# Turning two norms of a transformer block by DMA transposes instead of TensorE, with two-operand work freed for DVE

## The chip, the core and the metric

The kernel runs on one core of a Trainium2 chip. The core has TensorE (PE, matrix products, with weight loads shown apart as PEld), VectorE (DVE), ScalarE (ACT), GpSimd (POOL) and SyncE (SP, which here only issues DMAs). Every engine works through its own queue in order; they wait for each other through semaphores. TensorE writes to PSUM, the other engines read PSUM (POOL does not) and SBUF. The metric is the device time of one execution in microseconds.

## The reference

One transformer block on 2048 rows `x` of width 512, with a condition `c` that gives six vectors (shift, scale and gate for each of two halves):

```
mod = silu(c) @ w_mod                       # sa, ca, ga, sb, cb, gb
h = layernorm(x) * (1 + ca) + sa
q = h @ wq                                  # 32 heads of 128
p = softmax(q @ k^T / sqrt(128))            # the last 512 of 2048 cached keys
x = x + ga * ((p @ v) @ wo)
h = layernorm(x) * (1 + cb) + sb
x = x + gb * ((gelu(h @ w_gate) * (h @ w_up)) @ w_down)    # hidden width 1376
```

All inputs and outputs are float32.

## The kernel before

**Numbers.** A float32 value is kept as two float16 tiles, `high` (the rounded value) and `low` (the rest), and a product is three float16 matmuls: high x high, high x low, low x high. Making such a pair is an ACT copy to float16 and a subtraction. To fit float16's range every operand is scaled by its largest absolute value. For each group of two heads these maxima of four weights are *crossed* between partitions: `h_send` (L663) writes the 128 x 4 maxima to a small DRAM tile `most`, `spread_max` (L667) reads all 512 values back into every partition (tile `sa`), reduces them to four (`top`), scales them (`iv`) and takes the reciprocals (`av`). There are 29 such crossings, 28 for heads and one for the feed forward's weights; the first five sets of maxima go through TensorE instead.

**Work.** The 2048 rows are four groups (`qg`) of 512, and two pairs of groups (`p`). `acc` (16 tiles of 128 rows) is the running result. The attention runs 128 iterations (16 groups of heads x 4 row groups x 2 heads), each with scores (`psS`), the softmax, 512 DMA transposes in all from `pp` to `pT`, the product with `v` (`psO`) and with `wo` (`psW`), added to `acc`. From the third head group on, projections use a Strassen-Winograd scheme of seven products instead of eight for a pair of row groups, with the operand sums `T1` to `T4` beside the blocks `B11` to `B22`. The feed forward does the same: 20 units (besides the first pair's f = 0 and 1, which are done plainly), each a pair `p` and a hidden tile `f` of up to 128 columns, seven products of six matmuls into two `psS` tiles, then gelu, the gate, a split into `hid`, and the down projection into `psO`, `psW` or `psQ`, added to `acc`. The units of the first pair with f = 2 to 7 come first; the second pair's first unit is the seventh. Each unit also needs its weights loaded, scaled, summed (`S1` to `S4`) and split (`aw`), and these sums and splits are fixed on POOL.

**The second norm.** For a row group: `ln2_stats` (L1360) takes mean and variance, `ln2_norm` (L1363) writes the normalised rows in float32 to the tiles `N2` (in place of tiles no longer used, so the trace calls them `T` or `B`), and `ln2_chunk` (L1369) turns four 128 x 128 blocks on TensorE into a `psQ` bank, then applies scale and shift into `FULL`, with columns now on partitions. `ln2_high` and `ln2_low` split it into the views of `f_view` (L1354). For groups 1 to 3 `FULL` lives in one of two buffers of the tag `p32` (in the trace `hf`); for group 1 and group 3 these stay taken until `sums_a` and `sums_b` (L1800, L1811) have made the pair's sums and splits from them. The table `P1` (L1843) puts the second pair's norms, chunks and sums beside the units f = 2, 3 and 4 of the first pair.

**Order.** Nothing is issued at once. Every call notes an operation with its cost, its operands and, for some, two possible engines (`either`, L167); `tt` (L963) is a two-operand instruction that POOL or DVE can do, `affine` (L966) one that ACT or DVE can do. `issue` (L412) then plays the whole program in a model: it ranks the operations by how far from the end they have to be done, plays them forward, and repeats this 8 times and then with random shifts (drawn for every operation of the list in turn), stretch by stretch; the best play gives each queue its order and each operation its engine. In the model, a two-operand DVE instruction whose operands lie in SBUF, and any POOL instruction, take a shared lock; where both engines are possible, such an instruction on DVE is charged a penalty `SHY` of 1500 ns when engines are compared:

```
mine = max(t, shared[e] if kinds[e][1] else 0.0) + kinds[e][0] + (e == "DVE" and kinds[e][1]) * self.SHY
```

SP's queue is planned too, so loads and DMA transposes stand in one order. Every instruction is issued at L444, so the profile's rows are told apart by engine and tile.

Of the kernel before, what the change touches and what calls it, by code (L numbers as in the profile page):

```python
# [89 lines left out]
class Weaver:  # L90
# [159 lines left out]
    def play(self, at, users, span, keep, cut):  # L250
# [22 lines left out]
        def sooner(n, e, t):  # L273

            kinds = self.ops[n][4]
            mine = max(t, shared[e] if kinds[e][1] else 0.0) + kinds[e][0] + (e == "DVE" and kinds[e][1]) * self.SHY
            for o, kind in kinds.items():
                s = max(free[o], ready[n], shared[o] if kind[1] else 0.0)
                if o != e and s + kind[0] + (o == "DVE" and kind[1]) * self.SHY < mine:
                    return max(s, t) + 1.0  # L280
            return None

# [169 lines left out]
def adaln_block(ctx: ExitStack, tc: tile.TileContext, x, k_cache, v_cache, wq, wo,  # L452
# [17 lines left out]
    def small(pool, cols_, bufs=3, name="sm"):  # L470
        return pool.tile([P, cols_], F32, name=name, tag=name, bufs=bufs)
# [31 lines left out]
    def b_tile(p, nm, shape=(P, 2, 2, N), dtype=F16):  # L503
        return left1.tile(list(shape), dtype, name=f"{nm}_{p}", tag=f"{nm}_{p}", bufs=1)
# [30 lines left out]

    MV, RS, NMR, LNP, LNF = {}, {}, {}, {}, {}

    def ln_stats(key, src, j):
        if j == 0:
            MV[key] = base.tile([P, 4, 2], F32, name="mv", tag="mv", bufs=4)  # L540
            RS[key] = small(base, 4, 4, "rs")
        st = small(base, 6, 2, "bnst")
        nc.vector.bn_stats(st, src)
        nc.vector.bn_aggr(MV[key][:, j, :], st)
        if j == 3:
            ve = small(base, NC, 2, "ve")
            nc.gpsimd.tensor_tensor(ve, MV[key][:, :, 1], eps_t[:, :NC], op=OP.add)
            nc.gpsimd.tensor_tensor(RS[key], ve, eps_t[:, NC:], op=OP.pow)
            nm = NMR[key] = small(base, 4, 4, "nmr")
            nc.gpsimd.tensor_tensor(nm, MV[key][:, :, 0], RS[key], op=OP.mult)  # L550
            nc.gpsimd.tensor_scalar(nm, nm, -1.0, 1.0, op0=OP.mult, op1=OP.mult)
# [109 lines left out]
            IV[kh], AV[kh] = iv[:, i:i + 1], av[:, i:i + 1]  # L661

    def h_send(which, m):  # L663
        t = DG[which[0]] = dram.tile([P, 4], F32, name="most", tag="most", bufs=3)
        nc.sync.dma_start(t, m[:, 0:4])

    def spread_max(t, top):  # L667
        w = right.tile([P, N], F32, name="sa", tag="sa", bufs=1)
        nc.sync.dma_start(w, t.rearrange("p a -> (p a)").partition_broadcast(P))
        r = small(base, 4, 2, "top")  # L670
        nc.vector.tensor_reduce(r, w.rearrange("p (k a) -> p a k", a=4), op=OP.max, axis=AX.X)
        iv, av = small(base, 8, 5, "iv"), small(base, 8, 5, "av")
        nc.vector.tensor_scalar(iv[:, 0:4], r, 1e-30, ROUND / top, op0=OP.max, op1=OP.mult)
        nc.vector.reciprocal(av[:, 0:4], iv[:, 0:4])
        return iv, av

# [592 lines left out]
    def ff_scalars(part):  # L1269
        ab, t = ffs[:, 6:7], ffs[:, 7:8]  # L1270
        if part == 0:
            FS["iv"], av = spread_max(DG.pop("f"), WS)
            nc.vector.tensor_scalar_mul(ffs[:, 0:2], av[:, 0:2], 0.5)
            nc.vector.tensor_scalar_mul(ffs[:, 2:3], av[:, 2:3], 0.5)
            nc.vector.tensor_scalar(ab, FS["iv"][:, 3:4], WS, 1e-25, op0=OP.mult, op1=OP.max)
        iv = FS["iv"]
        if part == 1:
            nc.vector.tensor_scalar(ffs[:, 3:4], ab, iv[:, 0:1], 2.0 / HS, op0=OP.mult, op1=OP.mult)
            nc.vector.tensor_scalar(t, ab, iv[:, 0:1], 2.0, op0=OP.mult, op1=OP.mult)
            nc.vector.tensor_scalar(ffs[:, 5:6], ab, iv[:, 1:2], 4.0 * HID / HS, op0=OP.mult, op1=OP.mult)  # L1280
            nc.vector.tensor_scalar(ffs[:, 5:6], ffs[:, 5:6], iv[:, 2:3], t, op0=OP.mult, op1=OP.mult)
        if part == 2:
            nc.vector.tensor_scalar_mul(t, t, HID)
            nc.vector.reciprocal(ffs[:, 4:5], t)
            nc.vector.reciprocal(ffs[:, 8:9], ab)
            nc.vector.tensor_scalar(cols[:, 8:16], cols[:, 8:16], ffs[:, 8:9], HS, op0=OP.mult, op1=OP.mult)

    s = max(s, 2 * (NIT - 16))
# [49 lines left out]

    N2, FULL, FB, FRAW, AW, WD, WGU, PGU, HID_T, RT, UV, PX = ({} for _ in range(12))
    PLAIN = 2  # L1340
    SLOTS = ("q", "q", "q", "k16", "A1", "A1", "raw2", "raw2")
    SBUFS = {"q": 3, "k16": 1, "A1": 2, "raw2": 2}
    WDTAG = ("kT", "v", "wo", "kT", "kT", "v", "v", "wo", "wo", "oT", "oT")
# [14 lines left out]
        return t[:, 0, c % 2, :], t[:, 1, c % 2, :]  # L1358

    def ln2_stats(qg, j):  # L1360
        ln_stats(("2", qg), acc[4 * qg + j], j)

    def ln2_norm(qg, j):  # L1363
        if j % 2 == 0:
# [450 lines left out]
        f_low(p, c, "T4")  # L1815

    def chunk2(qg, c):
        ln2_chunk(qg, c)
        ln2_high(qg, c)
        ln2_low(qg, c, nc.vector)  # L1820

# [16 lines left out]
    for c in range(2):  # L1838
        sums_b(0, c)
    down_put(0, (0, 1))  # L1840


    P1 = {2: [(ln2_stats, 2, j) for j in range(4)] +  # L1843
          [(ln2_norm, 2, j) for j in range(4)] + [(chunk2, 2, c) for c in range(4)],
          3: [(ln2_stats, 3, j) for j in range(4)] +
          [(ln2_norm, 3, j) for j in range(4)] + [(chunk2, 3, c) for c in range(4)],
          4: [(sums_a, 1, c) for c in range(2)] + [(sums_b, 1, c) for c in range(2)]}
    WDS = list(range(PLAIN, NF))
    left = {(p, h): 2 if h < NF // 2 else 1 for p in range(2) for h in range(NF // 2 + 1)}
# [75 lines left out]
```

## Time and profile before

| what | us |
|---|---|
| median of 3 runs | 1657.21 (1657.04 to 1657.30) |
| the profiled execution | 1657.58 |
| its span | 1655.8 |
| PE busy in the span | 1642.4 |
| POOL, DVE, ACT busy | 1305.0, 1289.3, 1216.6 |

The terms of the page: `out<-in` names the tiles that an instruction writes and reads, with shapes as partitions x elements, then count, busy time and the mean of one in ns. Behind a bar stands the idle time of the engine just before these instructions, and what ended it. A row of a table by stretches gives the stretch, its length, each engine's busy time with its number of instructions, TensorE's granted clock, the mean busy share of the DMA engines and the GB/s they moved. A row about one tile gives the shortest, median and longest duration in ns and the first and last start. In a list in order of time, a line merges neighbours of one kind: start, length, engine. A row of waits gives the total, the count and the longest.

### The profile page before, as it was taken

How to read it: one execution, taken by the hardware profiler on the slowest of the kernel's cores; microseconds unless marked ns; L12 is line 12 of the kernel's file. 1: busy time of each engine (PE TensorE's matmuls, PEld its weight loads, DVE VectorE, ACT ScalarE, POOL GpSimd, SP SyncE). 2: the span in 40 equal slices, each digit the busy share in tenths (PEclk: the TensorE clock that was granted, in tenths of full speed). 3: DMA queues.
4: the chain of work that ended last, by engine and by line, in shares of the span. 5: the costliest groups of instructions: out<-in, count | busy, mean ns of one | idle time of the engine just before them, and what ended most of it. 6: DMA issues, size and time to landing. Idle time of an engine off the chain costs nothing.

```text
span 1655.8 us, 24293 instructions
## 1 busy us (share of the span) xinstructions
PE 1642.4 (99%) x7732; PEld 764.5 (46%) x7732; DVE 1289.3 (78%) x2381; ACT 1216.6 (73%) x2418; POOL 1305.0 (79%) x1097
## 2 busy tenths in 40 slices
PE   8999999999999999999999999999999999999999
PEld 4444444444444444444444444444444444444455
DVE  7777787878787788788999887888887956656557
ACT  5987797777787777888778777787878876545451
POOL 5999986868586878787768889999977898784682
PEclk9999999999999999999999999999999999999999
DMA  7676697878787778999999997788877712101111
GB/s 241 128 144 130 135 157 143 152 138 149 144 143 140 153 136 157 186 196 194 196 200 205 189 167 148 147 175 179 168 129 158 144 28 64 42 25 51 42 45 52
DMA packets 686289, 228.61 MB, mean 138 GB/s; under 512 B 596432, under 2 KB 663056, under 8 KB 686160
## 3 DMA queue, kind: packets, MB, share of 16 engines
q1 hardware_dynamic: 686160, 227.05, 69.1%
q8 instruction: 61, 1.00, 0.3%
q14 instruction: 68, 0.56, 0.1%
HBM read 78.98 MB, written 5.38 MB: 51 GB/s over the span
## 4 chain that ended last, share of the span: by engine, by line
PE 91%; ACT 2%; POOL 2%; DVE 2%; DMA 1%; SPq 1%; issue 1%; DVEq 0%; POOLq 0%; ACTq 0%
PE psS L444 31%; PE psW L444 23%; PE psO L444 21%; PE psQ L444 17%; SPq L444 1%; DVE st L444 1%; DVE acc L444 1%; DMA pT<-pp 1%; ACT p L444 0%; POOL pp L444 0%; POOL B L444 0%; DMA wm<-in_w_mod_dram 0%; POOL aw L444 0%; ACT T L444 0%; DMA raw<-in_B_w_up_dram 0%
## 5 line engine op out<-in xcount | busy, mean ns | idle before, releaser
L444 POOL TENSOR_TENSOR pp<-p,pp 128x1024 f16<-128x1024 f32 x256 | 545.9, 2132 | 212.8 <-ACT pp L444 97.3
L444 ACT ACTIVATE p<-psS,st,es 128x512 f32<-128x512 f32 x512 | 393.4, 774 | 187.7 <-DVE st L444 186.8
L444 DVE SCALAR_TENSOR_TENSOR acc<-psW,st,acc 128x512 f32<-128x512 f32 x496 | 367.2, 742 | 79.8 <-PE psW L444 77.7
L444 PE MATMUL psW<-wo,oT 128*128 128x512 f16 x1536 | 416.3, 379 | 0.0
L444 PE MATMUL psS<-kT,q 128*128 128x512 f16 x1536 | 379.1, 379 | 2.0 <-ACT q L444 2.0
L444 PE MATMUL psO<-pT,v 128*128 128x512 f16 x1536 | 377.1, 379 | 0.3 <-DMA pT<-pp 0.2
L444 DVE TENSOR_REDUCE st<-psS 128x2 f32<-128x1024 f32 x256 | 312.5, 1221 | 60.0 <-PE psS L444 59.6
L444 ACT ACTIVATE pp<-p 128x1024 f16<-128x1024 f32 x256 | 271.0, 1059 | 3.7
L444 PEld LDWEIGHTS <-q 128*128 128x128 f16 x1536 | 149.9, 98 | 182.1 <-ACT q L444 2.6
L444 PEld LDWEIGHTS <-v 128*128 128x128 f16 x1536 | 150.0, 98 | 181.3 <-DMA pT<-pp 1.2
L444 PEld LDWEIGHTS <-oT 128*128 128x128 f16 x1536 | 150.2, 98 | 180.1 <-DVE oT L444 0.5
L444 PEld LDWEIGHTS <-aw 128*128 128x128 f16 (+1 forms) x840 | 84.2, 100 | 95.1 <-issue 2.0
L444 ACT ACTIVATE oT<-psO 128x512 f16<-128x512 f32 x128 | 76.1, 594 | 66.2 <-PE psO L444 66.1
L444 PE MATMUL psQ<-T,S 128*128 128x512 f16 x504 | 123.3, 379 | 0.0
L444 PE MATMUL psQ<-B,A 128*128 128x512 f16 x480 | 119.6, 381 | 0.1
L444 PE MATMUL psS<-T,aw 128*128 128x512 f16 (+1 forms) x480 | 116.9, 379 | 0.0
L444 DVE SCALAR_TENSOR_TENSOR oT<-psO,oT 128x512 f16<-128x512 f32 x128 | 88.0, 688 | 30.9 <-ACT oT L444 30.6
L444 PEld LDWEIGHTS <-A 128*128 128x128 f16 x696 | 68.3, 98 | 83.3 <-issue 2.3
L444 PEld LDWEIGHTS <-S 128*128 128x128 f16 x672 | 65.8, 98 | 79.3
L444 ACT ACTIVATION_READ_ACCUMULATOR p<-psS,st,es 128x1 f32 x512 | 101.0, 197 | 0.0
L444 POOL TENSOR_TENSOR q<-h,q 128x512 f16<-128x512 f32 x84 | 97.5, 1161 | 2.0 <-ACT q L444 1.8
L444 DVE TENSOR_REDUCE mx<-raw 128x1 f32<-128x512 f32 x128 | 84.2, 674 | 15.6 <-DMA raw<-in_A_wq_dram 9.1
(211 smaller groups left out, 2295.6 us busy)
## 6 DMA issues: line engine op xcount, KB each, us to landing
raw<-in_A_k_cache_dram SPq DMA_DIRECT2D x32, 256.0 KB, 3.9
raw<-in_A_wq_dram SPq DMA_DIRECT2D x32, 256.0 KB, 3.7
raw<-in_A_v_cache_dram SPq DMA_DIRECT2D x32, 256.0 KB, 3.3
raw<-in_A_wo_dram SPq DMA_DIRECT2D x32, 256.0 KB, 3.2
pT<-pp SPq DMA_TRANSPOSE x512, 3.3
sa<-most SPq DMA_DIRECT2D x29, 256.0 KB, 3.8
raw<-in_B_w_gate_dram SPq DMA_DIRECT2D x24, 256.0 KB, 3.1
raw<-in_B_w_up_dram SPq DMA_DIRECT2D x24, 256.0 KB, 3.4
```

Of the source, the lines that this page charges most:

```text
L444: made[n] = real(*a, **k)
```

## The change

Three things are changed.

1. The norms of row groups 2 and 3 are turned by DMA. `turned_norm` normalises into a `p32` tile (scaled by 512 through `RS`, which `ln_stats` multiplies when `big` is set), and splits the row tile into a high and a low float16 half. `turned` issues two DMA transposes for each row tile, straight into the tiles that later hold the high and low parts. `turned_chunk` adds the two turned halves with scale and shift back into `FULL`: an `affine` on the low half, then a DVE instruction that multiplies the high half and adds. The chunk's split follows as before and overwrites the turned halves. `ffs[:, 9:13]` holds the scale for it.
2. The penalty `SHY` counts only for operations noted before `nc.calm`, the first of the feed forward's, so the feed forward's two-operand work goes to DVE or POOL by time alone.
3. The crossing's DRAM tile is 4 x 128 instead of 128 x 4, so a partition's four maxima are written as four single values, and each partition then reduces four runs of 128 neighbours. The scaling into `iv` goes from DVE to POOL.

```diff
@@ sooner
-            mine = max(t, shared[e] if kinds[e][1] else 0.0) + kinds[e][0] + (e == "DVE" and kinds[e][1]) * self.SHY
+            mine = max(t, shared[e] if kinds[e][1] else 0.0) + kinds[e][0] + (e == "DVE" and kinds[e][1]) * (self.SHY if n < self.calm else 0.0)
...
-                if o != e and s + kind[0] + (o == "DVE" and kind[1]) * self.SHY < mine:
+                if o != e and s + kind[0] + (o == "DVE" and kind[1]) * (self.SHY if n < self.calm else 0.0) < mine:
@@ ln_stats
+            if big:
+                nc.gpsimd.tensor_scalar(RS[key], RS[key], HS, 1.0, op0=OP.mult, op1=OP.mult)
@@ h_send, spread_max
-        t = DG[which[0]] = dram.tile([P, 4], F32, name="most", tag="most", bufs=3)
-        nc.sync.dma_start(t, m[:, 0:4])
+        t = DG[which[0]] = dram.tile([4, P], F32, name="most", tag="most", bufs=3)
+        nc.sync.dma_start(t.rearrange("a p -> p a"), m[:, 0:4])
...
-        nc.sync.dma_start(w, t.rearrange("p a -> (p a)").partition_broadcast(P))
+        nc.sync.dma_start(w, t.rearrange("a p -> (a p)").partition_broadcast(P))
...
-        nc.vector.tensor_reduce(r, w.rearrange("p (k a) -> p a k", a=4), op=OP.max, axis=AX.X)
+        nc.vector.tensor_reduce(r, w.rearrange("p (a k) -> p a k", a=4), op=OP.max, axis=AX.X)
...
-        nc.vector.tensor_scalar(iv[:, 0:4], r, 1e-30, ROUND / top, op0=OP.max, op1=OP.mult)
+        nc.gpsimd.tensor_scalar(iv[:, 0:4], r, 1e-30, ROUND / top, op0=OP.max, op1=OP.mult)
@@ ff_scalars
+            nc.vector.tensor_scalar_mul(ffs[:, 9:13], cols[:, 8:12], ffs[:, 8:9])
@@ the feed forward
+    nc.calm = len(nc.ops)
...
-        ln_stats(("2", qg), acc[4 * qg + j], j)
+        ln_stats(("2", qg), acc[4 * qg + j], j, qg in TURNED)
+
+    TURNED = (2, 3)
+
+    def turned_norm(qg, j):
+        if j % 2 == 0:
+            t = b_tile(0, N2TAG[qg][j // 2], (P, 2, 2, 2, N // 2))
+            N2[qg, j], N2[qg, j + 1] = t[:, 0], t[:, 1]
+            RT["norm"] = right.tile([P, 2, N], F32, name="hf", tag="p32", bufs=2)
+        n, t = RT["norm"][:, j % 2, :], N2[qg, j]
+        nc.either((S_, V), lambda o: ln_norm(("2", qg), n, acc[4 * qg + j], j, o))
+        n = n.rearrange("p (a n) -> p a n", a=2)
+        nc.scalar.activation(t[:, :, 0, :], n, AF.Copy)
+        tt(t[:, :, 1, :], n, t[:, :, 0, :], OP.subtract)
+
+    def turned(qg, j):
+        for half in range(2):
+            nm = (("B11", "B21"), ("T4", "B22"))[qg % 2][half]
+            d = ff_b(qg // 2, nm).rearrange("p a c n -> p (a c) n")
+            nc.sync.dma_start_transpose(d[:, :, j * P:(j + 1) * P], N2[qg, j][:, half].rearrange("p a n -> p (a n)"))
+
+    def turned_chunk(qg, c):
+        if c % 2 == 0:
+            RT["full"] = right.tile([P, 2, N], F32, name="hf", tag="p32", bufs=2)
+        full = FULL[qg, c] = RT["full"][:, c % 2, :]
+        a, b = ffs[:, 9 + c:10 + c], colB[2][:, c:c + 1]
+        hi, lo = f_view(qg, c)
+        affine(full, lo, a, b)
+        nc.vector.scalar_tensor_tensor(full, hi, a, full, op0=OP.mult, op1=OP.add)
@@ chunk2 and P1
-        ln2_chunk(qg, c)
+        turned_chunk(qg, c)
...
-          [(ln2_norm, 2, j) for j in range(4)] + [(chunk2, 2, c) for c in range(4)],
+          [(g, 2, j) for j in range(4) for g in (turned_norm, turned)] + [(chunk2, 2, c) for c in range(4)],
...
-          [(ln2_norm, 3, j) for j in range(4)] + [(chunk2, 3, c) for c in range(4)],
+          [(g, 3, j) for j in range(4) for g in (turned_norm, turned)] + [(chunk2, 3, c) for c in range(4)],
```

2 lines of the change are left out of this document (1 added, 1 removed).

## The prediction

> **What bounds the kernel now.** I read the page's first part first, then busy time by stretch, then TensorE's waits in the tail, then the instructions on the tile `ident` (the transposes), then the groups of the stretch in which the changed code runs.
>
> ```profile
> span 1655.8 us, 24293 instructions
> PE 1642.4 (99%) x7732; PEld 764.5 (46%) x7732; DVE 1289.3 (78%) x2381; ACT 1216.6 (73%) x2418; POOL 1305.0 (79%) x1097
> ```
>
> ```profile
> core 0: us, PE busy (x) PEld busy (x) DVE busy (x) ACT busy (x) POOL busy (x), PEclk, DMA share, GB/s
> 0.00:50.00 50.00, 42.42 (x203) 24.88 (x204) 37.91 (x97) 30.76 (x53) 29.70 (x51) 0.93 0.73 216
> ...
> 400.00:600.00 200.00, 200.00 (x928) 90.69 (x927) 161.59 (x307) 151.44 (x308) 144.07 (x109) 1.00 0.78 146
> ...
> 1300.00:1350.00 50.00, 49.40 (x245) 24.39 (x244) 40.34 (x79) 41.65 (x77) 42.74 (x42) 1.00 0.51 106
> 1350.00:1400.00 50.00, 50.00 (x247) 24.40 (x245) 28.79 (x43) 36.55 (x67) 43.23 (x52) 1.00 0.14 37
> 1400.00:1450.00 50.00, 49.95 (x234) 22.82 (x233) 32.83 (x42) 27.41 (x50) 40.93 (x42) 1.00 0.20 56
> 1450.00:1500.00 50.00, 49.09 (x227) 22.10 (x226) 29.60 (x40) 25.10 (x47) 38.35 (x44) 1.00 0.11 31
> 1500.00:1550.00 50.00, 50.00 (x234) 23.70 (x232) 31.11 (x42) 27.41 (x54) 29.23 (x37) 1.00 0.14 38
> ```
>
> TensorE is busy in every microsecond of the attention stretches and has a full granted clock there: 928 instructions in 200 us are 0.2155 us each, the pace of a 512-column matmul. It is idle 7.6 us in the first 50 us and about 1.5 us in the feed forward (0.6 us before 1350, 0.9 us after 1450). What it waits for from 1290 us on:
>
> ```profile
> PE psS L444 <- POOL B L444: 0.6, 1, 0.6
> PE psS L444 <- ACT r L444: 0.5, 1, 0.5
> PE psS L444 <- DVE r L444: 0.4, 1, 0.4
> ```
>
> So the kernel is TensorE's queue plus a start and an end. An edit shortens the time by the TensorE work that it takes out, and by no more than 1.5 us through waits in the feed forward; it lengthens the time by every wait that it puts in. Work that leaves DVE, ACT or POOL is worth nothing by itself.
>
> **What the change removes.** `ln2_chunk` transposes row groups 2 and 3 on TensorE, 2 groups x 4 chunks x 4 tiles = 32 instructions. They are these, and one group of four stands between matmuls like this:
>
> ```profile
> L444 PE MATMUL psQ<-ident,T x32: 272/273/328, 1353.3 to 1416.7; 128*128 128x128 f32 x32
> ```
>
> ```profile
> 1355.51 0.65 PE L444 MATMUL psQ<-ident,T 128*128 128x128 f32 x4
> 1356.00 1.24 PE L444 MATMUL psS<-B,aw 128*128 128x512 f16 x5
> ...
> 1358.59 0.60 PE L444 MATMUL psQ<-ident,T 128*128 128x128 f32 x4
> 1359.03 0.38 PE L444 MATMUL psS<-B,aw 128*128 128x512 f16 x1
> ```
>
> The 273 ns of one is its length in a pipeline. Its cost is the distance to the next start: 0.44 us for four here, and 0.49 us for the group at 1355.51. Eight such groups are 3.5 to 3.9 us; most look like the 0.44 one, so I take 3.6 us. No TensorE instruction is added. The profiled execution took 1657.58 us (span 1655.8 us and 1.8 us around it), so with a full queue it would take 1654.0 us; the median of the runs shown is 0.4 us below the profiled one, so the forecast stands against 1657.21 us: 1657.21 - 3.6 = 1653.6 us.
>
> **What it adds in the feed forward.** The rows are from 1350 to 1460 us, where both norms, their chunks and the sums of the second pair run:
>
> ```profile
> L444 DVE TENSOR_TENSOR hid<-r,hid 128x512 f16<-128x512 f32 x14 | 12.2, 880 | 2.0 <-ACT hid L444 1.9
> L444 DVE SCALAR_TENSOR_TENSOR r<-r,ffs 128x512 f32<-128x512 f32 x12 | 11.2, 956 | 0.1
> L444 POOL TENSOR_TENSOR T<-hf,T 128x512 f16<-128x512 f32 x9 | 10.9, 1213 | 1.3 <-DVE r L444 0.6 <-DVE hid L444 0.6
> L444 POOL TENSOR_TENSOR B<-hf,B 128x512 f16<-128x512 f32 x6 | 6.9, 1163 | 1.9 <-DVE hid L444 1.9
> L444 ACT ACTIVATE raw<-raw,ffs 128x512 f32<-128x512 f32 x9 | 6.2, 708 | 0.0
> L444 ACT ACTIVATE T<-acc,nmr,rs 128x512 f32<-128x512 f32 x6 | 4.5, 803 | 0.8 <-POOL nmr L444 0.8
> L444 ACT ACTIVATE T<-hf 128x512 f16<-128x512 f32 x7 | 4.4, 622 | 2.2 <-POOL hf L444 2.2
> L444 ACT ACTIVATE hf<-psQ,cols 128x512 f32<-128x512 f32 x4 | 3.1, 778 | 1.7 <-POOL B L444 1.4 <-PE psQ L444 0.3
> ```
>
> For each of the 8 row tiles `turned_norm` adds an ACT copy (622 ns) and a two-operand subtraction (1163 ns on POOL; on DVE 880 ns in this stretch, 686 ns where nothing held it up, below). For each of the 8 chunks `turned_chunk` keeps the affine, now from SBUF (708 to 803 ns instead of 778), and adds a DVE instruction with two SBUF operands (686 to 956 ns). That is 5.0 us of ACT, 5.5 to 9.3 us for the subtractions and 5.5 to 7.6 us of DVE, over some 75 us. ACT has 36 us idle in the 100 us from 1350, DVE 38 us, POOL 16 us: the sum fits if some of POOL's work goes to DVE, which the removed penalty lets the planner do. On TensorE's path none of it costs anything as long as the second pair's operands are ready in time.
>
> ```profile
> L444 DVE TENSOR_TENSOR hid<-r,hid 128x512 f16<-128x512 f32 x6 | 4.0, 686 | 0.0
> ```
>
> ```profile
> 1354.68 0.78 ACT L444 ACTIVATE hf<-psQ,cols 128x512 f32<-128x512 f32 x1
> ...
> 1362.87 0.81 DVE L444 TENSOR_SCALAR hf<-psQ,cols 128x512 f32<-128x512 f32 x1 [3.56 <-PE psW L444]
> ```
>
> ```profile
> 1409.05 2.28 POOL L444 TENSOR_TENSOR B<-hf,B 128x512 f16<-128x512 f32 x2 [0.63 <-DVE hid L444]
> ...
> 1459.25 1.16 POOL L444 TENSOR_TENSOR T<-hf,T 128x512 f16<-128x512 f32 x1
> ```
>
> **The longer chain.** The norms now go through the two `p32` buffers, which hold the first pair's chunks until its sums are done. They came free for the next chunks at about 1354.7 and 1362.9 us, so the second two norms of group 2 start at about 1363. Estimated from the rows above: two norms, copies and subtractions 5 us, turning 4 us, two chunks of a buffer 5 us; the same again for group 3 gives 28 us, ready at about 1391. The trace of before splits group 3's chunks from 1409 on and finishes the sums' splits at 1460, so the latency fits with some 18 us to spare.
>
> ```profile
> L444 SPq DMA_TRANSPOSE pT<-pp x512: 1231/1326/4018, 42.7 to 1320.1; - x171
> ```
>
> ```profile
> pT<-pp SPq DMA_TRANSPOSE x512, 3.3
> most<-mx SPq DMA_DIRECT2D x28, 2.0 KB, 1.9
> msu<-mall SPq DMA_DIRECT2D x2, 2.0 KB, 3.1
> ```
>
> ```profile
> 1419.92 12.37 SPq L444 DMA_DIRECT2D raw<-in_B_w_down_dram  x3
> ```
>
> The 16 DMA transposes are half as long as the 512 known ones, so each takes between 0 and 1.33 us of SP (I take 0.7) and lands in at most 3.3 us after issue; the DMA engines are used at 0.11 to 0.20 here. A transpose that waits on SP for its subtraction holds back the weight loads behind it, and the loads themselves wait for buffers (three of them across 12.4 us at 1420), which could hold a transpose back; the loads run two units ahead and the chain has its 18 us, so I price both at nothing; if that cover were gone, a transpose behind such a load would cost up to the 12.4 us of that row.
>
> **The crossings.** 29 times, under attention:
>
> ```profile
> L444 DVE TENSOR_REDUCE top<-sa x29: 1061/1080/1159, 160.5 to 1221.8; 128x4 f32<-128x512 f32 x29
> L444 DVE TENSOR_SCALAR iv<-top x29: 134/164/633, 168.3 to 1224.9; 128x4 f32<-128x4 f32 x29
> ```
>
> ```profile
> L444 DVE TENSOR_REDUCE mx<-raw x128: 622/675/687, 15.8 to 1212.8; 128x1 f32<-128x512 f32 x128
> ```
>
> Laid out by kind, the reduction reads neighbours like `mx<-raw`: between no gain and 0.4 us, and I take 0.4. The scaling leaves DVE for POOL, 0.16 us, and the reciprocal on DVE then waits for POOL, behind up to one 1.2 us subtraction. The send now writes 512 single values instead of 128 runs of four; the nearest row that moves single values is `msu<-mall` (3.1 us) against 1.9 us, so it lands 0 to 1.2 us later. The DMA engines are busy enough elsewhere for this to be taken up: 0.78 in the row of 400 to 600. All of it lies under stretches in which TensorE lost nothing in 200 us, and the heads are prepared a group ahead; I price it at nothing, and at -0.2 to +1 us if one crossing comes too late.
>
> **The redrawn order.** The list of operations and DVE's penalty change, so the planner's search draws another order for all queues. The start's 7.6 us of idle can come out otherwise: I allow 1 us either way (the longest waits there are about that), and take 0.
>
> **The rivals.**
> (1) *Waits come back at the second pair* (a wait takes the place of the work removed). DVE empties `psS` and `psW` in order; the three waits quoted above already end on ACT's and DVE's `r`. Each two-operand instruction given to DVE stands ahead of such an emptying for 0.7 to 1.0 us, and five of them that come at the wrong moment return half of the gain: 1653.6 + 2 = 1655.6 us, with 1 to 5 us as its spread. For it speaks DVE's mean of 880 and 956 ns against 686; against it, that TensorE lost only 0.9 us with these.
> (2) *The port that DVE's two-operand instructions and POOL take in turns is full, and the time rises.* In 1350 to 1460 POOL is busy 43.2 + 40.9 + about 8 = 92 of 110 us, and DVE's 26 instructions of the two quoted groups need 18 us even at 686 ns: 110 of 110. The change adds 11 to 17 us. Every POOL instruction moved to DVE returns 1.16 - 0.69, about 0.5 us. If half of the addition isn't returned, 8 us arrive late at the second pair's first unit, whose last splits end at 1460 already with no spare: 1653.6 + 8 = 1661.6 us. It decides from the point where the last `T` split ends later than about 1465. Against it: POOL is busy only 29 us in 1500 to 1550, so weight splits can slide past it.
> The Trainium skill, "SBUF — State Buffer", "Who interferes with whom", says that a DVE instruction with two SBUF inputs and a GpSimd instruction that reads SBUF exclude each other for a whole instruction. The rows agree (686 against 880 ns), and by that rule DVE's idle time is not free for this work: it is what rival 2 works out.
> (3) *The gain is larger*: the 1.5 us of waits go too, since DVE does a subtraction in less time than POOL, or the start comes out 1 us shorter: 1653.6 - 2 = 1651.6 us.
> (4) That the transposes stay on TensorE can't be: the chunks of groups 2 and 3 call nothing that issues them.
>
> **How the numbers follow.** Forecast with a full queue 0.55 (own range 1652.6 to 1654.6), rival 1 0.22, rival 2 0.11, rival 3 0.12. About 0.2% (3.3 us, so below 1653.9 or above 1660.5) is what a measurement of this kernel tells from no change. The forecast lies only 0.3 us beyond that line: two thirds of it, 0.37, and all of rival 3 count as faster, 0.49; the remaining 0.18 and rival 1 are the same, 0.40; rival 2 is slower, 0.11. The range takes in rival 3's centre and rival 1's spread and stops short of rival 2's centre: 1651.6 to 1658.6.
>
> **What would show it.** Right: no `psQ<-ident` after 1345 us, TensorE idle in the feed forward at 2 us or less, its busy time lower by 3 to 4 us, half or more of the `T`, `B` and `ft` subtractions on DVE. Wrong: a wait of `psS` on `r`, `T` or `B` of over 1 us near the second pair (rivals 1 and 2), or a start that differs by more than 1 us from 42.4 us busy in 50.

## The result, and the profile after

| | median us (range) |
|---|---|
| before, run beside it | 1657.12 (1656.26 to 1657.30) |
| the changed kernel | 1783.67 (1782.28 to 1788.34) |
| ratio, 95% interval | 1.077 (1.0754 to 1.0786) |

The change costs 126 us. The profiled execution took 1782.98 us. The page's first part, then its stretches and one crossing in a table by stretches, with the columns as before:

```profile
span 1781.2 us, 24348 instructions
PE 1673.3 (94%) x7700; PEld 766.3 (43%) x7700; DVE 1438.6 (81%) x2642; ACT 1224.1 (69%) x2424; POOL 1035.0 (58%) x857
```

```profile
400.00:500.00 100.00, 93.16 (x418) 41.43 (x417) 77.15 (x146) 68.47 (x142) 54.87 (x40) 0.97 0.79 135
900.00:1000.00 100.00, 85.35 (x384) 37.85 (x383) 74.15 (x137) 66.35 (x135) 53.52 (x36) 0.94 0.88 140
...
1500.00:1550.00 50.00, 50.00 (x234) 22.68 (x232) 39.73 (x57) 35.19 (x68) 29.33 (x35) 1.00 0.31 72
```

The 32 transposes are gone (7700 against 7732) and POOL's work has moved to DVE (1438.6 against 1289.3, 1035.0 against 1305.0), so the change does what it says. But the loss lies under attention, where TensorE had been busy in every microsecond: 418 and 384 matmuls in 100 us, where the full pace is 464. The feed forward is fast again. The added 125.4 us of span (1781.2 - 1655.8) split into 94.5 us more of TensorE's idle time (107.9 against 13.4) and 30.9 us more of its busy time, in spite of 32 fewer instructions.

What TensorE, POOL and DVE wait for (rows of waits over the whole span):

```profile
POOL iv L444 <- DVE top L444: 79.2, 18, 10.4
...
DVE top L444 <- DMA sa<-most: 75.5, 20, 7.6
...
PE psO L444 <- DMA pT<-pp: 34.2, 17, 5.8
...
PE psQ L444 <- DVE q L444: 27.1, 7, 7.7
...
PE psW L444 <- DVE acc L444: 24.6, 15, 3.8
```

Two rows of waits of the kernel before, the second for later:

```profile
DVE mx L444 <- DMA raw<-in_A_wq_dram: 9.1, 5, 2.2
DVE top L444 <- DMA sa<-most: 7.2, 8, 2.2
```

DVE now stands before the crossing's reduction 20 times, for up to 7.6 us, and what DVE should empty meanwhile (`q`, `acc`) is late for TensorE. The transfers, with their median from issue to landing in us, say where this begins:

```profile
most<-mx SPq DMA_DIRECT2D x28, 2.0 KB, 9.5
...
B<-T SPq DMA_TRANSPOSE x12, 2.5
...
T<-T SPq DMA_TRANSPOSE x4, 2.4
```

The crossing's send, 1.9 us before, lands after 9.5 us. One crossing in order of time:

```profile
629.87 0.57 SPq L444 DMA_DIRECT2D most<-mx  x1
...
631.13 2.62 SPq L444 DMA_TRANSPOSE pT<-pp  x2
...
641.34 0.33 SPq L444 DMA_DIRECT2D sa<-most  x1
...
642.21 0.38 PE L444 MATMUL psO<-pT,v 128*128 128x512 f16 x1 [3.35 <-DMA pT<-pp]
...
645.71 0.69 DVE L444 TENSOR_REDUCE top<-sa 128x4 f32<-128x512 f32 x1 [7.61 <-DMA sa<-most]
```

```profile
630.00:634.00 4.00, 4.00 (x21) 1.81 (x19) 3.84 (x10) 2.52 (x6) 1.16 (x1) 1.00 0.79 135
634.00:638.00 4.00, 4.00 (x20) 1.81 (x19) 3.25 (x7) 4.00 (x9) 3.22 (x3) 1.00 1.68 31
638.00:642.00 4.00, 0.86 (x4) 0.20 (x2) 0.11 (x1) 0.88 (x2) 2.93 (x2) 1.00 1.28 63
642.00:646.00 4.00, 3.79 (x18) 1.79 (x19) 0.29 (x1) 0.00 (x0) 0.00 (x0) 1.00 1.48 188
```

SP issues the send at 629.9 and two transposes at 631.1, and then, but for one load, nothing until 641.3: the read of `most` stands next in its queue and waits for the send. The two transposes were issued before that, and still TensorE can use the last one only at 642.2, some 8.5 us after SP was done with it at 633.75; the median of such a transfer is 3.3 us, and the longest of the changed kernel 14.8 us (6.8 before):

```profile
DMA to landing us min/median/max: 3.1/3.3/14.8
```

In the table the last two columns are the share of the DMA engines and the GB/s that they moved. The share is the time that the packets took, added up, so it can pass 1: from 634 to 638 it is the highest of these rows (1.68), with 31 GB/s. Few packets, each of them long, fit a send that does not only land late but holds up other transfers while it does.

### The profile page after: what moved, and what is told of

Read it like the earlier page. It is cut to its first block, busy times and chain, and to the rows that moved or that the text cites. A ratio compares the mean times of both kernels' runs of the same rounds, so it can differ in the third digit from the quotient of the medians.

```text
span 1781.2 us, 24348 instructions
## 1 busy us (share of the span) xinstructions
PE 1673.3 (94%) x7700; PEld 766.3 (43%) x7700; DVE 1438.6 (81%) x2642; ACT 1224.1 (69%) x2424; POOL 1035.0 (58%) x857
## 5 line engine op out<-in xcount | busy, mean ns | idle before, releaser
L444 PE MATMUL psW<-wo,oT 128*128 128x512 f16 x1536 | 474.2, 384 | 25.8 <-DVE acc L444 24.6
L444 PE MATMUL psO<-pT,v 128*128 128x512 f16 x1536 | 409.2, 383 | 37.5 <-DMA pT<-pp 34.2
L444 PE MATMUL psS<-kT,q 128*128 128x512 f16 x1536 | 411.3, 384 | 1.2 <-ACT q L444 1.2
L444 PE MATMUL psQ<-T,S 128*128 128x512 f16 x504 | 144.0, 395 | 27.2 <-DVE q L444 27.1
L444 PE MATMUL psQ<-B,A 128*128 128x512 f16 x480 | 129.2, 380 | 1.2 <-DVE h L444 1.1
L444 PE MATMUL psS<-T,aw 128*128 128x512 f16 (+1 forms) x480 | 121.1, 379 | 0.0
L444 PE MATMUL psS<-B,aw 128*128 128x512 f16 (+1 forms) x360 | 90.0, 379 | 0.0
```

The lines of the kernel that those rows point to most:

```text
L444: made[n] = real(*a, **k)
```

## The experiments

**Part by part.** The first runs take each part alone or leave the suspect out. The crossing's layout alone, in the kernel before:

```diff
-        t = DG[which[0]] = dram.tile([P, 4], F32, name="most", tag="most", bufs=3)
-        nc.sync.dma_start(t, m[:, 0:4])
+        t = DG[which[0]] = dram.tile([4, P], F32, name="most", tag="most", bufs=3)
+        nc.sync.dma_start(t.rearrange("a p -> p a"), m[:, 0:4])
...
-        nc.sync.dma_start(w, t.rearrange("p a -> (p a)").partition_broadcast(P))
-        nc.vector.tensor_reduce(r, w.rearrange("p (k a) -> p a k", a=4), op=OP.max, axis=AX.X)
+        nc.sync.dma_start(w, t.rearrange("a p -> (a p)").partition_broadcast(P))
+        nc.vector.tensor_reduce(r, w.rearrange("p (a k) -> p a k", a=4), op=OP.max, axis=AX.X)
```

> The kernel before with the crossing's new layout alone (4 x 128, single values sent, four runs reduced); scaling on DVE, penalty and norms as before. Theory L (the send of 512 single values lands after 9.5 us in the trace of after, not after 1.9 us as before, and SP, DVE and POOL stand in order behind it): 1735 to 1785 us, the send again near 9 us. Theory S (the penalty's removal reaches the attention, because its operations are noted after the line that sets the border: POOL has 857 instructions instead of 1097, and DVE's extra work delays what empties PSUM): 1655 to 1662 us, late sends or not.

Measured: 1804.84 us against 1657.46, ratio 1.0885 (1.0869 to 1.0901). The next kernel is the changed one with these lines turned back (`iv` stays on POOL):

> The changed kernel with the crossing's old layout (128 x 4), all else as changed: scaling on POOL, penalty off, norms turned. Theory L: 1653 to 1670 us, the send at 2 us, no long waits of DVE on the spread maxima. Theory S: 1730 to 1785 us, with TensorE's waits on DVE's q and acc left as they are.

Measured: 1661.15 us, ratio 1.0019 (1.0009 to 1.0028). The other two parts alone, in the kernel before: the penalty taken off as in the change, and the turned norms with the penalty kept, the old layout and `iv` on DVE.

```diff
-            ... (e == "DVE" and kinds[e][1]) * self.SHY
+            ... (e == "DVE" and kinds[e][1]) * (self.SHY if n < self.calm else 0.0)
+    nc.calm = len(nc.ops)
```

> The kernel before with the penalty off for all operations noted from the feed forward's set-up on, as in the change; nothing else. Theory S: 1700 us or more. Theory L: 1650 to 1668 us; POOL's instructions fall to about 860 as in the changed kernel, and TensorE stays busy all the same, with at most 10 us of waits on DVE.

```diff
-    nc.calm = len(nc.ops)
+    nc.calm = 1 << 30
```

> The kernel before with the turned norms alone: old crossing with its scaling on DVE, penalty on everywhere. Both theories: the prediction's own step, TensorE's queue 3.6 us shorter, 1653.6 us; up to 1657 us if the longer chain brings waits at the second pair, since without DVE's help the subtractions stay on POOL.

Measured: penalty off alone 1671.55 us, ratio 1.0080 (1.0065 to 1.0095); turned norms alone 1671.94 us, ratio 1.0086 (1.0069 to 1.0103). The pages of these two kernels:

```profile
most<-mx SPq DMA_DIRECT2D x28, 2.0 KB, 9.4
```

```profile
most<-mx SPq DMA_DIRECT2D x28, 2.0 KB, 2.1
...
PE 1638.2 (99%) x7700; PEld 760.7 (46%) x7700; DVE 1446.3 (87%) x2642; ACT 1223.9 (74%) x2424; POOL 1035.9 (62%) x857
```

The first row is of the layout alone, the other two are of the change without it. With the layout goes the send's 9.4 us and 147 us; without it both are gone, and the change costs 3.7 us. So the layout makes some 122 of the 126 us. Neither of the other parts gains anything alone: each loses 14 us, and together they lose less than either. The extra 21 us by which the layout alone is slower than the whole change were not taken apart.

**Late or in the way?** The planner's model has a small DMA land some 2.5 us after issue when no other is under way. If the loss comes from queues laid out for an early landing (SP and DVE standing in order behind a late value), a planner that knows of the 8 us lays the reads later and wins most of it back. If the send disturbs other transfers, it can't.

```diff
-                end = bus + 650.0
+                end = bus + 650.0 + 8000.0 * (n in self.slow)
```

with `slow` the sends of `most`, and the same 8000 ns added where the model ranks the operations from the end.

> The changed kernel, whose planner is told that the crossing's send lands 8 us later than it assumes; the sends stay 512 single values. Theory Q (the time is lost because instructions stand in order behind a send that the plan believes landed: SP's read of it ahead of DMA transposes, DVE's reduction, POOL's scaling): 1655 to 1675 us, the sends still at 9 us, few waits of DVE on the spread maxima. Theory D (the sends' many small writes slow the DMA engines and so the transposes themselves, whoever waits): 1730 us or more.

Measured: 1792.80 us, ratio 1.0806 (1.0767 to 1.0845), no better than 1783.67. Its rows of waits:

```profile
DVE mx L446 <- DMA raw<-in_A_wq_dram: 50.1, 11, 10.4
...
DVE top L446 <- DMA sa<-most: 28.4, 12, 5.3
...
PE psW L446 <- DVE acc L446: 41.7, 14, 8.9
...
PE psO L446 <- DMA pT<-pp: 23.3, 11, 4.8
```

DVE's wait for the crossing fell from 75.5 to 28.4 us, as the planner now leaves room. SP's own wait for the send, 70.5 us in the changed kernel, is gone altogether. The time did not fall with them: DVE waits for weight loads instead (50.1 us; 9.1 us before the change). That speaks for transfers in each other's way. What the packets of the trace show, lined up on the issue of every send (all traffic but packets of 16 bytes and less, the mean over 29 sends):

```
us from the send's issue     -4..0   0..4   4..8   8..12   12..16
before, GB/s                   160    123    175     156      151
after, GB/s                    163    110     59      77      201
planner told, GB/s             175     99     44      70      185
longest packet of the other transfers in 4..8 us (median of the 29 sends):
0.59 us before, 2.67 us after, 2.35 us with the planner told
```

From 4 to 12 us after the issue the other transfers move a third to a half of what they moved at that place before. The rate alone would not prove that they are held up, since SP issues little while it stands behind the send. The length of the packets is less open to that: the longest are some four times what they were, also in the kernel where SP no longer waits for the send. The send's own packets are short: in the crossing shown they take up to 9 ns each, all within half a microsecond after 631.0; the long ones are the transposes' of 256 bytes.

**Which writes are slow?** Unread extra sends in the kernel before, beside the crossing's own; they add work and leave none out. In the first kernel every crossing issues three kinds back to back; in the second each crossing issues one, four kinds in turn:

```diff
         nc.sync.dma_start(t, m[:, 0:4])
+        # in turn, each to a DRAM tile of its own:
+        prk: [4, 128]      <- m[:, 0:4]   512 values, 128 neighbours at 4 B
+        prs: [128, 8]      <- m[:, 0:4]   512 values, at 8 B
+        prw: [4, 128 x 16] <- m[:, 0:4]   512 values, at 64 B
+        pro: [1, 128]      <- m[:, 0:1]   128 values, neighbours at 4 B
```

> The kernel before with three more sends at each of the 28 crossings of heads, which nobody reads: prk (512 single values laid out by kind, as in the change), prs (512 single values, a partition's four 8 bytes apart in 32 bytes of its own), pro (128 single values, one kind). If single values cost by their number, prk and prs both land after about 9 us, pro after 2 to 3 us. If it is neighbours from different partitions in one line of DRAM, prk and pro are slow against prs, which lands after about 2 to 4 us. The time itself: 1657 to 1700 us, of no weight.

> The kernel before with one more unread send at each crossing of heads, of four kinds in turn, seven of each: prk (512 single values by kind, neighbours 4 bytes apart in DRAM), prs (512 single values, 8 bytes apart), prw (512 single values, 64 bytes apart), pro (128 single values, 4 bytes apart). In the first probe all three stood behind one another and landed together at 9 to 11 us, which told nothing apart. If the number of values decides: prk, prs, prw near 9 us, pro near 3 us. If neighbours in one line of DRAM decide: prw 2 to 4 us, prk, prs and pro slow. Time between 1700 and 1800 us, of no weight.

Measured, one execution each: 1894.06 us for the first and 1733.91 us for the second. In the first, `pro`, `prs` and `prk` land after 9.2, 9.4 and 10.6 us in the median. The landings in the second:

```profile
most<-mx SPq DMA_DIRECT2D x28, 2.0 KB, 2.1
...
prk<-mx SPq DMA_DIRECT2D x8, 2.0 KB, 9.5
...
prs<-mx SPq DMA_DIRECT2D x7, 2.0 KB, 4.6
...
prw<-mx SPq DMA_DIRECT2D x7, 2.0 KB, 2.6
...
pro<-mx SPq DMA_DIRECT2D x6, 0.5 KB, 9.2
```

In the first kernel the three kinds are issued back to back and all read about alike, so it tells nothing of a kind by itself. The second does. 512 single values cost 2.6 us when each has 64 bytes to itself, and 128 single values cost 9.2 us when they are neighbours. So it is not the number of single values but how closely they are written. Counted by the packets that fall into the same 64 bytes, 1, 4 (the old layout's 16-byte runs), 8 and 16 of them give 2.6, 2.1, 4.6 and 9.2 to 9.5 us: from 4 up the time is about 0.6 us for each. That is a fit to five rows, in which the 64 bytes are a choice; it looks as if packets to the same place in DRAM were written one after the other, which no run shows by itself.

The Trainium skill, "DMA: Bandwidth & Descriptors", "Specifications", says that transfers of less than 512 bytes cost a read-modify-write. By that, the old layout's 16 bytes and the new one's 4 would both pay it; the runs (2.1 against 9.5 us, and 2.6 us for 4 bytes apart from each other) show a difference that this rule alone does not give. Its "Rules for kernel authors" speaks against this change: a non-contiguous last dimension becomes one descriptor per element and should be made contiguous. The changed send is such a case and is slow, but the send of 512 single values 64 bytes apart is one too, and lands in 2.6 us: the count of descriptors alone is not the price.

**The turned norms and the penalty.** What remains is 3.7 us, though each of the two other parts alone loses 14. First the border: in the changed kernel `nc.calm` stands at L1344, but the attention's operations are noted later, by the loop `for i in range(NIT + 4): slot(i)` (L1825); the penalty is off for the attention too. These two kernels set the border behind that loop, the first with the turned norms, the second without:

```diff
-    nc.calm = len(nc.ops)
...
         slot(i)
+    nc.calm = len(nc.ops)
     hooks(
```

> The kernel before with the turned norms, and the penalty off from the feed forward's own operations on (the border noted behind the attention's loop); old crossing, scaling on DVE. If the 12 us that the turned norms alone lose in 1400 to 1500 us come from POOL's share of the subtractions, they shrink to 0 to 3 us and the attention loses nothing: 1652 to 1657 us. If the longer chain through two buffers and SP's queue is what is late, 1662 us or more, as with the turned norms alone.

> The kernel before with the penalty off in the feed forward alone; norms turned on TensorE, old crossing. If POOL's share is what the feed forward's 1.5 us of waits rest on: 1655 to 1657 us. If DVE's added work delays what empties PSUM, as it did in the attention when the penalty was off there (14 us): 1659 us or more.

Measured: with the turned norms 1659.90 us, ratio 1.0014 (1.0005 to 1.0023); without them 1667.06 us, ratio 1.0059 (1.0044 to 1.0074). So taking the penalty off costs 14.1 us where it goes for the attention too and 9.9 us where it goes behind it, and the same freedom in the feed forward is worth 12 us once the turned norms are in (1671.94 to 1659.90).

Where the first two losses lie is seen from TensorE's instructions between 200 and 1300 us, under attention: 5095 before, 5019 with the penalty off everywhere, 5062 with it off in the feed forward alone. At 0.2155 us each that is 16 us, as much as the whole loss of 14, and 7 of the 9.9 us, though in the second kernel the attention keeps its penalty. In the change without the layout it is 5076, some 4 us lost, with the penalty off as in the first. The turned norms have no work there, so they can't be what brings 16 us down to 4: the redrawn order can, or `iv` on POOL, and no run tells these apart.

Why do the turned norms lose? By the prediction's own candidates: the buffers `p32`, the two-operand work, or the new draw of the order. The norms through a tile of their own:

```diff
-            RT["norm"] = right.tile([P, 2, N], F32, name="hf", tag="p32", bufs=2)
-        n, t = RT["norm"][:, j % 2, :], N2[qg, j]
+        n, t = ga, N2[qg, j]
```

> The kernel with turned norms and the penalty off in the feed forward alone, whose norms go through the tile of the attention's gate (free by then) instead of the two p32 buffers. If the p32 buffers make the second pair late (the chain of norms and chunks through the same two buffers), TensorE's loss in 1400 to 1500 us falls from 5.8 us to 2 us or less: 1654 to 1656.5 us. If it is the sheer work on POOL, DVE and ACT, nothing changes: 1658 to 1662 us.

> The turned norms with the penalty on everywhere, through the gate's tile instead of the p32 buffers. If the buffers are the cause: from 1672 us to 1655 to 1660 us. If it is POOL's work (eight more subtractions, kept there by the penalty): 1668 to 1675 us.

Measured: 1659.78 us, ratio 1.0015 (1.0006 to 1.0025), where the penalty is off in the feed forward, and 1670.60 us, ratio 1.0078 (1.0061 to 1.0095), with the penalty. Both are where they were: the buffers are not the cause. The work itself, with the penalty on: the low halves left out, so no subtraction and no instruction on DVE that adds the halves (the second pair is then computed from rows rounded to float16, and only the high half is transposed), and the turned norms for one group only:

```diff
-        tt(t[:, :, 1, :], n, t[:, :, 0, :], OP.subtract)
...
-        affine(full, lo, a, b)
-        nc.vector.scalar_tensor_tensor(full, hi, a, full, op0=OP.mult, op1=OP.add)
+        affine(full, hi, a, b)
```

> The turned norms with the penalty on, without the low halves: no subtraction when a row tile is split, only the high half turned, and the chunk made from it by the affine instruction alone, so the second pair is computed from rounded rows. What is left is the chain: norm, copy, DMA transpose, chunk, through the same buffers and SP's queue. If the 16 added two-operand instructions are what makes the second pair late (alone the turned norms lost 17 us in 1400 to 1500): 1653 to 1658 us. If the chain through the DMA transposes is: 1665 to 1673 us.

```diff
-    TURNED = (2, 3)
+    TURNED = (3,)
```

> The turned norms for row group 3 alone, penalty on; group 2 on TensorE as before. TensorE's queue is 1.8 us shorter. If the loss goes with the added work: half of it, 1660 to 1666 us. If it comes only past a point (POOL just full): 1655 to 1659 us. If group 3's place at the end of the chain makes it: 1668 us or more.

Measured: 1655.13 us, ratio 0.9983 (0.9973 to 0.9992), without the low halves; 1662.44 us, ratio 1.0026 (1.0015 to 1.0037), with one group. The last split of `T` before the change, then stretches and the last split of `T`, first of the turned norms with the penalty, then of the same without low halves:

```profile
1463.61 1.16 POOL L444 TENSOR_TENSOR T<-ft,T 128x512 f16<-128x512 f32 x1
```

```profile
1400.00:1450.00 50.00, 43.55 (x192) 18.77 (x191) 32.70 (x42) 31.05 (x53) 38.79 (x42) 0.97 0.40 88
1450.00:1500.00 50.00, 44.07 (x193) 19.14 (x193) 29.75 (x36) 25.25 (x47) 39.85 (x39) 0.97 0.09 26
```

```profile
1477.92 1.16 POOL L444 TENSOR_TENSOR T<-ft,T 128x512 f16<-128x512 f32 x1 [0.56 <-ACT T L444]
```

```profile
1400.00:1450.00 50.00, 48.59 (x225) 21.89 (x224) 29.92 (x41) 37.93 (x67) 39.58 (x43) 1.00 0.26 67
1450.00:1500.00 50.00, 48.65 (x226) 21.92 (x225) 28.91 (x40) 26.21 (x49) 36.59 (x42) 1.00 0.11 31
```

```profile
1461.99 1.16 POOL L444 TENSOR_TENSOR T<-ft,T 128x512 f16<-128x512 f32 x1
```

```profile
PE 1638.6 (99%) x7700; PEld 761.5 (46%) x7700; DVE 1294.0 (78%) x2377; ACT 1240.4 (75%) x2455; POOL 1286.4 (78%) x1075
```

In the same 100 us TensorE does 385 matmuls with the low halves and 450 without; before the change it did 460. At full pace 385 take 83 us, so some 17 us are lost with them. The last split ends 14 us later than before with them, and is in time without them. The transposes, half as long without them, hold SP as long (1.24 against 1.26 us each) and land in 2.3 instead of 2.5 us, so their length is not what changes.

So the added two-operand work is what costs, with the penalty on. It does not reach TensorE as a wait for the second pair's operands: no row of TensorE's waits names `T` or `B` there. With the low halves, from 1395 to 1505 us (TensorE's own waits are 12.3 us in all):

```profile
ACT wd L444 <- POOL raw L444: 4.6, 4, 2.4
...
PE psW L444 <- ACT wd L444: 3.7, 2, 2.2
PE psW L444 <- DVE acc L444: 3.6, 2, 3.2
```

```profile
1431.07 2.27 POOL L444 TENSOR_TENSOR T<-hf,T 128x512 f16<-128x512 f32 x2
...
1435.40 1.22 SPq L444 DMA_TRANSPOSE T<-T  x1
...
1437.97 1.52 ACT L444 ACTIVATE hf<-T,cols,ffs 128x512 f32<-128x512 f16 x2 [5.68 <-DMA T<-T]
1438.81 0.75 DVE L444 SCALAR_TENSOR_TENSOR hf<-T,ffs,hf 128x512 f32<-128x512 f16 x1 [5.27 <-ACT hf L444]
...
1440.28 1.24 PE L444 MATMUL psW<-wd,hid 128*128 128x512 f16 x5 [3.15 <-DVE acc L444]
```

SP's transposes wait for ACT's copies and POOL's subtractions (6.3 and 4.9 us between 1395 and 1445) and then go out one behind the other. ACT and DVE, each in order, stand 5.7 and 5.3 us before the turned tile, and TensorE stops for the `acc` of a unit of the first pair that stands behind it. Another part is POOL's late `raw`, from which ACT makes `wd`. The path changes with the order: with another draw (below) ACT stands before the same tile for 4.4 us, while with the tile of their own there is no such wait, and the longest stop, 5.3 us, ends on ACT's `r`. POOL is busy 79 of 100 us here, 79 before the change and 76 without the low halves: how full it is does not tell these kernels apart, only what waits behind it. Whether the subtractions or DVE's added halves weigh more isn't taken apart.

**The draw.** Since every change of the list redraws the order, three kernels are planned with another start of the random numbers (`random.Random(8)` in place of 7): the kernel before, the turned norms with the penalty, and those with a tile of their own and the penalty off in the feed forward.

> The kernel before, with another seed for the planner's random shifts: what a redrawn order alone does. The prediction allowed 1 us either way: 1656 to 1658.5 us. If redrawing is worth several us, up to 1665 us, and a single pair of kernels can't show a step of 3.6 us.

> The turned norms alone (penalty on, old crossing) with another seed of the planner's shifts. If the 14.5 us of the turned norms are one unlucky draw: 1653 to 1660 us. If they are the work's: 1667 to 1675 us.

> Turned norms through the gate's tile, penalty off in the feed forward alone, with the other seed: the best case for a version that beats the kernel before. If the losses under attention in the first two such kernels (2 to 4 us) are a matter of the draw: 1654 to 1657 us. If the feed forward still loses 3 us or more: 1657 to 1662 us.

Measured: 1658.35 us, ratio 1.0004 (0.9995 to 1.0014); 1669.42 us, ratio 1.0073 (1.0057 to 1.0090); 1658.34 us, ratio 1.0010 (1.0001 to 1.0020). A draw is worth up to 2.5 us in these three pairs; with the penalty off for the attention no other draw was run. The 14 us of the turned norms with the penalty are not the draw; of the 2 to 4 us that remain where the penalty is off, a good part may be.

`iv` on POOL was not run alone. No run that computes all that the kernel computes was faster than the kernel before.

## Why the prediction was wrong, point by point

The forecast was 1653.6 us, 3.6 us less than before; measured were 1783.67 us, 126 us more.

**The crossings: the step that failed.** The prediction put the send 0 to 1.2 us late, from the row `msu<-mall`, and priced the whole at nothing. It measured 7.6 us late (9.5 against 1.9) and 122 us. That row is a read of single values into SBUF partitions; the send writes single values to neighbouring DRAM addresses, which no row of before showed. An unseen operation was taken between near bounds. The cover failed as well: the row of 400 to 600, in which TensorE lost nothing, says that there was no wait, not how late a transfer could be before there was one. And the send was priced as if it were alone; that it takes the transposes' and the loads' bandwidth away was in no step and no rival. That the disturbed transfers carry the loss fits three measurements (the table of GB/s, the transposes at 631, the planner told of the delay); how writes to neighbouring addresses hold up the others inside the DMA engines or the memory, no run shows.

**The reduction.** Taken at 0.4 us less from `mx<-raw`, and so it is (1080 ns before, 687 ns at most after):

```profile
L444 DVE TENSOR_REDUCE top<-sa x29: 655/686/687, 157.1 to 1350.5; 128x4 f32<-128x512 f32 x29
```

But TensorE was the bound and not DVE, and no run shows a gain from these 0.4 us.

**TensorE's 3.6 us.** This step was right: busy time fell from 1642.4 to 1638.2 us without the layout, and to 1638.6 us without the low halves, where the median fell by 2.5 us. It is the only part of the change for which a run shows a gain, and the forecast was nothing but it.

**The added work in the feed forward: the second step that failed.** It was priced at nothing on the ground that the sum of idle times holds it "if some of POOL's work goes to DVE". With the penalty on, the low halves' work costs 16.8 us (1671.94 against 1655.13); the turned norms lose 14.5 us in all, with one group 4.8. Rival 2 (1661.6 us, a chance of 0.11) named this work as the cause and was the better forecast of the norms, 8 us of delay against some 17 us lost between 1400 and 1500. Its mark came true: the last `T` split starts at 1477.9, later than about 1465. But the mark is a soft one. The split at 1459.25, which the prediction took for the last before, is followed by the one at 1463.61, and the change without the layout has its last at 1467.1 without a wait for it. And its path, the second pair waiting for its splits, is not the one seen: TensorE waits for the first pair's `acc` and `wd`, held up where ACT and DVE stand in order behind a turned tile and where POOL is late. That the queues of ACT and DVE carry a late turned tile on to TensorE was in no step and no rival. The rule of the Trainium skill, "SBUF — State Buffer", "Who interferes with whom", that such DVE and GpSimd instructions exclude each other, agrees with the 686 and 880 ns of the prediction's rows; none of these runs measures the exclusion by itself.

**The latency through the buffers.** The two buffers were not the cause: a tile of their own changed 1659.90 to 1659.78 and 1671.94 to 1670.60. But the estimate, all turned by about 1391, failed. In the turned norms with the penalty the transposes run to 1438:

```profile
L444 SPq DMA_TRANSPOSE B<-T x12: 1188/1257/2417, 1401.1 to 1438.0; - x12
```

In the change without the layout, too, the last starts at 1436.4, and there it does little harm. The estimate added up durations and left out the waits in the queues of POOL, ACT and DVE.

**The penalty.** The description before the prediction, and with it the prediction, took it as lifted for the feed forward alone. It is lifted for the attention too, and the step to check was the order in which operations are noted, not the place of the line. With the border behind the attention it costs 9.9 us without the turned norms, of which some 3 us lie in the feed forward. Rival 1 had 2 us (1 to 5) for DVE's two-operand instructions standing ahead of the emptying of PSUM at the second pair; its five instructions of 0.7 to 1.0 us come to 3.5 to 5 us by themselves. The waits of the kernel with the penalty off are of this kind, but under attention, 9.3 us in these two rows:

```profile
PE psW L444 <- DVE acc L444: 6.2, 7, 1.9
...
PE psQ L444 <- DVE q L444: 3.1, 3, 1.7
```

In the change both losses are smaller: 14 and 14 apart, 3.7 together. The turned norms need the freedom in the feed forward (12 us); why the freedom under attention costs less in the change is open. That the net is near nothing fits the forecast's price for these two parts by luck: its reason, that neither costs anything, was wrong.

**SP's queue.** Priced at nothing. The 16 new transposes land in 2.4 to 2.5 us in the median (at most 3.3 was said) and hold SP for 1.2 to 1.3 us each, not 0.7. From 1280 us on, TensorE waits for no transpose in the kernel without the layout; in the turned norms with the penalty ACT does, for 5.7 us, as shown above.

**The order.** The allowance of 1 us either way for a new draw was near for the kernel before (0.8 us) and small for the others (up to 2.5 us).

**What was to be seen.** TensorE's count and its busy time without the layout are as foretold, and so is DVE's share; in the changed kernel from 1440 us on:

```profile
L444 DVE TENSOR_TENSOR T<-hf,T 128x512 f16<-128x512 f32 x17 | 12.1, 727 | 0.0
...
L444 POOL TENSOR_TENSOR T<-hf,T 128x512 f16<-128x512 f32 x3 | 3.5, 1158 | 1.4 <-DVE T L444 1.4
```

The mark "no `psQ<-ident` after 1345" was a bad one: the longer attention moved the first pair's transposes, which stay, to 1436.9 to 1468.2. A mark in absolute time fails when what lies ahead of it changes. The sign of being wrong at the start came true (40.68 us busy in 50 against 42.42), but the loss doesn't lie there.

## What to carry to other kernels

Price a DMA by the addresses that it writes as well as by its bytes: if the trace has no row of the same pattern, its cost has no upper bound from rows that look alike, and the price must include what the transfer does to its neighbours. Where one engine's idle time is to hide new work, count what shares a port or lock with it in the very stretch; when that count comes out full, take the case seriously, however much idle time each engine shows alone, and ask what stands in order behind the late result on every engine that uses it. Two edits that each move work between the same two engines are to be costed together.

## What the runs showed of the hardware

**Small writes.** From issue to landing: 2.1 us for 128 runs of 16 bytes, 2.6 us for 512 single values at 64 bytes, 4.6 us at 8 bytes, 9.5 us at 4 bytes, and 9.2 us for 128 single values at 4 bytes. From 4 to 12 us after the issue of such a send in the changed kernel, the other transfers move 59 and 77 GB/s (175 and 156 before), and the longest packet among them takes 2.67 us in the median, 0.59 us before.

**TensorE's clock falls with the stops.** A stretch of the changed kernel, ahead of the crossing shown:

```profile
615.00:625.00 10.00, 7.56 (x28) 2.83 (x26) 4.90 (x9) 3.93 (x10) 2.12 (x1) 0.83 0.89 168
```

By the trace's record of the clock, half rate was granted in 16 stretches, 77.7 us in all, after the change (15 of 3.4 or 6.8 us, one of 2.6 us at the end), and in 2 stretches, 10.6 us, before it. TensorE was busy for 61.0 and 6.3 us of them. Half of the difference is 27 us, most of the 34.5 us by which the busy time rose (the 30.9 us of added busy time and the 3.6 us that the transposes took out); the other 7 us are not accounted for. So of the 125 us of span about three quarters are stops, and most of the last quarter is the slow clock that follows them. The Trainium skill, "TensorE: Matmul & The Clock Gate", "What's actually happening", says that the gate goes back to half rate after an idle window of about 3.4 us. The lengths of the stretches, multiples of 3.4 us, agree with a window of that length. The stops do not give a threshold: those that end at 524.07 and 834.74 us last 2.1 us, and a half-rate stretch begins within 0.5 us of their end, while the one of 3.35 us that ends at 642.21 us has none after it for 8 us. Where they differ, the measurement stands: a stop of 2.1 us can be enough, and an edit that brings in such stops pays for them twice.
